# Decode attention on one core: 896 B of unused SBUF ahead of the tile that all loads write

## The chip, the cores and the metric

The kernel runs on one core of one Trainium2 chip. Its time is the device time of one execution in microseconds (us); three runs of the kernel before gave 1961.86, 1964.46 and 1965.69 us, with a median of 1964.46.

## The reference

Two independent attention blocks, A and B, each a decode step: one query token per sequence, two sequences, 32 heads with 192 elements each, and a cache of 8192 keys and values per head. The two outputs of 640 columns stand side by side. Everything is bf16.

```python
def _B_ref(x, k_cache, v_cache, wq, wo):          # x [2,1,640], caches [2,32,8192,192]
    B, Sq, D = x.shape
    H, Dh = 32, 192
    q = (x @ wq).reshape(B, Sq, H, Dh).transpose(0, 2, 1, 3)
    scores = jnp.einsum("bhqd,bhkd->bhqk", q, k_cache) * (Dh ** -0.5)
    p = _softmax(scores, axis=-1)
    o = jnp.einsum("bhqk,bhkd->bhqd", p, v_cache)
    return o.transpose(0, 2, 1, 3).reshape(B, Sq, H * Dh) @ wo
```

Block A computes the same with its own inputs. The four caches hold 201 MB each, so some 837 MB pass from DRAM through the core once, the weights included, and each value of a cache is used for one multiplication.

## The kernel before

**Units and loads.** A unit is one pair of heads of one sequence in one block: 64 units (`NU`). Its K (and likewise its V) is one load of 128 partitions x 128 tokens x 192 elements: the first head's 8192 tokens lie in partitions 0 to 63, the second head's in 64 to 127, so that each partition receives one contiguous row of 49152 B. A load is 6144 KB. SyncE issues all of them in one queue in the order K0, K1, V0, K2, V1, ... (`loads`), after the two query weights `wq` (61440 B per partition each). The output weights `wo` come at the end, in eight pieces (`pieces`), beside the last V, which is cut in three (`VCUT`).

**One tile holds everything that is loaded.** `big` (declared at line 136) is 172032 B in each partition: three buffers of 49152 B for K and V in turn (`kv`), and two buffers of 12288 B for products (`prod`). The weights `wq` and `wo` and the input x are loaded into the same bytes before and after they serve K and V. A buffer's next load waits until the load that lay in it has been used (`done`): a K until its last multiplication, a V until its last matmul.

**A unit's work.** VectorE multiplies a quarter of K by the unit's query (`dve_mul`, L280, four per unit, 128x6144 elements each) into a `prod` buffer. TensorE adds the 192 products of each token down to 16 partial sums with twelve matmuls against the identity (`pe_sum`, L352), and VectorE adds those 16 (`dve_red`, L283). GpSimd takes the maximum over the partitions (L261), ScalarE the exponential (L317), and TensorE multiplies the probabilities by V in 64 matmuls (`pe_pv`, L365). The queries are made at the start (L344), and the output projection (L387) runs at the end.

**Order.** Every engine's instructions are put in a table by unit (`put`) and emitted in that order; semaphores order the engines among each other. TensorE's steady part is a loop over six units.

**Places in SBUF.** Tiles are laid out in the order in which they are declared. Ahead of `big` lie 16384 B that the DMA machinery keeps and four small constants at 32 B each, so `big` begins at byte 16512 of each partition, which is 16 x 1024 + 128. Behind it come the queries (`qall`), the probabilities (`pb`), the scores (`sc`) and smaller tiles, up to byte 227944 of 229376.

The offsets inside `big` at which loads begin are multiples of 1024 B (the buffers at 0, 49152 and 98304; the second `wq` at 110592; pieces of `wo` at 30720, 20480, 10240 and 15360 from a buffer's start), save for the two small loads of x (at 100864) and the last piece of `wo` (at 17920 from a buffer's start), which begin 512 B past one.

Of the kernel before, what the change touches and what calls it, by code (L numbers as in the profile page):

```python
# [8 lines left out]
BF16 = mybir.dt.bfloat16  # L9
# [94 lines left out]
def build_kernel(nc, blocks, out):  # L104
# [26 lines left out]
    with ExitStack() as es:  # L131
        sb = lambda name, shape, dt: es.enter_context(nc.sbuf_tensor(name, shape, dt))
        ps = lambda name, shape, dt: es.enter_context(nc.psum_tensor(name, shape, dt))
        sem = lambda name: es.enter_context(nc.semaphore(name))

        big = sb("big", [128, NBUF * BUFE + 2 * PRODE], BF16)
        qall = sb("qall", [128, NU, Dh], BF16)
        pb = [sb(f"pb{i}", [128, TJ, MP], BF16) for i in range(2)]
# [389 lines left out]
def bass_concat_heads__gqa_block_cached__mha_block_cached__decode_kernel(  # L528
    nc: bass.Bass,
    A_x: bass.AP,  # L530
    A_k_cache: bass.AP,
    A_v_cache: bass.AP,
    A_wq: bass.AP,
    A_wo: bass.AP,
    B_x: bass.AP,
    B_k_cache: bass.AP,
    B_v_cache: bass.AP,
    B_wq: bass.AP,
    B_wo: bass.AP,
    out: bass.AP,  # L540
):
    blocks = [
        dict(x=A_x, k=A_k_cache, v=A_v_cache, wq=A_wq, wo=A_wo),
        dict(x=B_x, k=B_k_cache, v=B_v_cache, wq=B_wq, wo=B_wo),
    ]
    build_kernel(nc, blocks, out)
# [28 lines left out]
```

## Time and profile before

| what | value |
|---|---|
| median of three runs | 1964.46 us |
| the profiled execution | 1963.75 us |
| its span, first to last instruction | 1962.0 us |
| TensorE busy | 1527.6 us, 78% |
| VectorE busy | 1123.5 us, 57% |
| ScalarE, GpSimd busy | 160.3 and 31.3 us |
| read from DRAM | 836.77 MB, 426 GB/s over the span |
| mean granted TensorE clock | 0.949 |

Times of the profile count from the start of the span. A line of instruction groups gives the source line, the engine, the operation, what it writes and reads, and how often, then the busy time in us and the mean of one in ns. A line of a stretch gives its bounds and length, each engine's busy time with the number of instructions, the granted clock, the busy share of the 16 DMA engines and GB/s. A line of the chain or of the timeline begins with its start and its length in us. A chain is followed back from the last instruction: it names, for each moment, what the work that ended last was waiting for. A DMA in it lasts from its issue to its landing, queueing included.

### The profile page before, as it was taken

Reading aid. Unit: us, or ns where it says so; the run is one execution under the profiler, and the core shown is the slowest. Engines: PE = TensorE matmul, PEld = TensorE weight load, DVE = VectorE, ACT = ScalarE, POOL = GpSimd, SP = SyncE. Lnnn points to the kernel's source line nnn. Section 1 sums busy time; section 2 is a strip of 40 time slices with the busy share of each in tenths; the row PEclk is TensorE's granted clock in tenths of the full one; section 3 lists DMA queues with packets and bytes.
Section 4 is the critical chain, followed back from the end, with each engine's and each line's share of the span. In section 5 each row is a group of like instructions: output and inputs, shape, how many; then the busy total and the mean of one; then the engine's idle time right before and its main releaser. Section 6 shows DMA issues by size and latency. Waiting matters only on the chain.

```text
span 1962.0 us, 17861 instructions
## 1 busy us (share of the span) xinstructions
PE 1527.6 (78%) x7781; PEld 744.5 (38%) x7781; DVE 1123.5 (57%) x901; ACT 160.3 (8%) x519; POOL 31.3 (2%) x80
## 2 busy tenths in 40 slices
PE   4787877877877787777787787787787787777888
PEld 2343433333333333333333343343343343333345
DVE  3865565565565565566556556556556556556540
ACT  3100000000000000000000000000000000000000
POOL 1000000000000000000000000000000000000000
PEclk9999999999999988999998999999999898999899
DMA  9999999999999999999999999999999999999977
GB/s 396 433 433 432 433 432 432 433 433 433 431 433 433 433 433 433 433 433 433 433 432 433 432 433 433 432 433 433 433 434 433 433 433 433 433 433 432 433 332 327
DMA packets 20212, 837.12 MB, mean 427 GB/s; under 512 B 2252, under 2 KB 2264, under 8 KB 2648
## 3 DMA queue, kind: packets, MB, share of 16 engines
q1 hardware_dynamic: 20164, 836.77, 98.9%
q8 instruction: 13, 0.21, 0.0%
q14 instruction: 15, 0.12, 0.0%
q10 hardware_dynamic: 20, 0.01, 0.0%
HBM read 836.77 MB, written 0.01 MB: 426 GB/s over the span
## 4 chain that ended last, share of the span: by engine, by line
DMA 49%; PE 30%; DVE 20%; issue 0%; ACT 0%; SPq 0%
DMA big<-in_B_k_cache_dram 24%; DMA big<-in_A_k_cache_dram 22%; DVE big L280 17%; PE ops L365 17%; PE scps L352 11%; DVE sc L283 2%; DMA big<-in_B_wq_dram 2%; PE outps L387 1%; DMA big<-in_B_v_cache_dram 1%; PE scps L344 1%; PE ops L358 0%; PE oTps L374 0%; ACT out_sb L327 0%; SPq L235 0%; DVE mp L289 0%
## 5 line engine op out<-in xcount | busy, mean ns | idle before, releaser
L280 DVE TENSOR_TENSOR big<-big,qall 128x6144 bf16<-128x6144 bf16 x256 | 852.7, 3351 | 534.3 <-DMA big<-in_B_k_cache_dram 277.4
L352 PE MATMUL scps<-big,ident 128*128 128x512 bf16 x3072 | 782.2, 412 | 402.1 <-DVE big L280 402.1
L365 PE MATMUL ops<-big,pb 128*34 128x384 bf16 x4096 | 678.5, 327 | 3.7 <-DMA big<-in_B_v_cache_dram 3.7
L352 PEld LDWEIGHTS scps<-big,ident 128*128 128x128 bf16 x3072 | 304.0, 104 | 873.7 <-DVE big L280 497.8
L365 PEld LDWEIGHTS ops<-big,pb 128*34 128x34 bf16 x4096 | 396.0, 98 | 263.6 <-DMA big<-in_B_v_cache_dram 3.8
L283 DVE TENSOR_REDUCE sc<-scps 128x32 f32<-128x512 f32 x256 | 175.9, 687 | 206.6 <-PE scps L352 206.6
L309 ACT ACTIVATE nb<-mg 64x1 f32<-64x1 f32 x128 | 25.7, 201 | 1705.0 <-POOL mg L261 1704.3
L317 ACT ACTIVATE pb<-sc,nb 64x128 bf16<-64x128 f32 x128 | 81.7, 638 | 3.1
L261 POOL PARTITION_ALL_REDUCE mg<-mp x64 | 25.9, 405 | 1860.4 <-DVE mp L289 1860.4
L344 PE MATMUL scps<-big 128*128 128x384 bf16 x160 | 31.1, 364 | 14.5 <-DMA big<-in_A_wq_dram 11.0
L317 ACT ACTIVATION_READ_ACCUMULATOR pb<-sc,nb 64x1 f32 x128 | 38.5, 301 | 0.0
L289 DVE TENSOR_REDUCE mp<-sc 64x1 f32<-64x128 f32 x128 | 35.9, 280 | 3.1
L270 DVE CAST qall<-scps 64x192 bf16<-64x192 f32 x64 | 22.7, 355 | 19.5 <-PE scps L344 16.8
L303 ACT ACTIVATE qall<-o_sum,rc 2x192 bf16<-2x192 f32 x64 | 29.0, 454 | 18.1 <-DVE o_sum L300 16.4
L344 PEld LDWEIGHTS scps<-big 128*128 128x128 bf16 x160 | 17.1, 108 | 28.2 <-DMA big<-in_A_wq_dram 11.1
L387 PE MATMUL outps<-big,oTz 128*4 128x320 bf16 x192 | 26.6, 299 | 0.7 <-ACT out_sb L327 0.7
L294 DVE RECIPROCAL rc<-ops 2x1 f32<-2x1 f32 x64 | 10.0, 156 | 28.3 <-PE ops L365 26.3
L274 ACT ACTIVATE qall<-scps 64x192 bf16<-64x192 f32 x64 | 20.8, 325 | 34.4 <-DVE qall L270 32.2
L297 DVE COPY o_hi<-ops 2x192 f32<-2x192 f32 x64 | 22.3, 349 | 2.0
L300 DVE TENSOR_TENSOR o_sum<-ops,o_hi 2x192 f32<-2x192 f32 x64 | 22.1, 346 | 2.2
L387 PEld LDWEIGHTS outps<-big,oTz 128*4 128x4 bf16 x192 | 16.1, 85 | 10.7 <-issue 1.2
L358 PEld LDWEIGHTS ops<-ones,rs 128*2 128x2 f32 x128 | 5.5, 82 | 26.8 <-issue 26.7
(24 smaller groups left out, 42.0 us busy)
## 6 DMA issues: line engine op xcount, KB each, us to landing
big<-in_A_k_cache_dram SPq DMA_DIRECT2D x32, 6144.0 KB, 29.2
big<-in_A_v_cache_dram SPq DMA_DIRECT2D x32, 6144.0 KB, 28.1
big<-in_B_k_cache_dram SPq DMA_DIRECT2D x32, 6144.0 KB, 29.1
big<-in_B_v_cache_dram SPq DMA_DIRECT2D x31, 6144.0 KB, 27.9
big<-in_A_wq_dram SPq DMA_DIRECT2D x1, 7680.0 KB, 21.7
big<-in_B_wq_dram SPq DMA_DIRECT2D x1, 7680.0 KB, 39.8
big<-in_A_wo_dram SPq DMA_DIRECT2D x2, 3840.0 KB, 23.3
big<-in_B_wo_dram SPq DMA_DIRECT2D x2, 2560.0 KB, 32.1
```

Of the source, the lines that this page charges most:

```text
L261: return lambda eng: eng.partition_all_reduce(mg[u % 2][:], mp[u % 2][:], 128, bass.bass_isa.ReduceOp.max)
L270: return lambda eng: eng.tensor_copy(qall[ro, B * hp + 1 - s, :], qps[hp % NCH][ri, s * Dh:(s + 1) * Dh])
L280: return lambda eng: eng.tensor_tensor(prod[c % 2], t[:, c * TC:(c + 1) * TC, :], q, ALU.mult)
L283: return lambda eng: eng.tensor_reduce(sc[u % 2][:, c * TC:(c + 1) * TC], scps[c][:], AXL.X, ALU.add)
L289: ins = eng.tensor_reduce(mp[u % 2][r, s:s + 1], sc[u % 2][r, :], AXL.X, ALU.max)
L303: return lambda eng: eng.activation(qall[0:2, u, :], o_sum[:], ACTF.Identity, scale=rc[u % 2][:])
L309: ins = eng.activation(nb[u % 2][r, :], mg[u % 2][r, s:s + 1], ACTF.Identity, scale=-scale)
L317: ins = eng.activation(pb[u % 2][r, :, s::32], sc[u % 2][r, :].rearrange("p (j a) -> p j a", a=2), ACTF.Exp, bias=nb[u % 2][r, :], scale=s ...
L344: ins = eng.matmul(qps[hp % NCH][:, 0:QW], xbc[:, blk, c, :], wq_t[blk][:, c, off:off + QW], start=(c == 0), stop=(c == DC - 1))
L352: ins = eng.matmul(scps[c][:], ident[:], prod[c % 2][:, :, j * DG:(j + 1) * DG], start=(j == 0), stop=(j == NJ - 1))
L365: ins = eng.matmul(ops[u % 2][0:MP, 0:QW], pb[u % 2][:, j, :], vv[:, j, :], start=(j == 0), stop=(j == TJ - 1))
L387: ins = eng.matmul(outps[0:4, 0:NH2], oTz[blk][:, i, 2 - 2 * half:6 - 2 * half], wo[:, i - r0, half * NH2:(half + 1) * NH2], start=(i == 0 ...
```

## The change

One unused tile is declared ahead of `big`. It takes 448 bf16 elements, 896 B, in each partition. `big` then begins at byte 17408 = 17 x 1024, and all tiles behind it lie 896 B higher, the last one ending at byte 228840 of 229376. Nothing reads or writes the new tile.

```diff
@@ -133,6 +133,7 @@
         ps = lambda name, shape, dt: es.enter_context(nc.psum_tensor(name, shape, dt))
         sem = lambda name: es.enter_context(nc.semaphore(name))
 
+        shift = sb("shift", [128, 448], BF16)
         big = sb("big", [128, NBUF * BUFE + 2 * PRODE], BF16)
         qall = sb("qall", [128, NU, Dh], BF16)
         pb = [sb(f"pb{i}", [128, TJ, MP], BF16) for i in range(2)]
```

Every instruction stays in its place on its engine; only addresses in SBUF differ. The line numbers of the changed kernel are one higher.

## The prediction

> **What bounds the kernel now.** First the slices of the page, then the queue, then the stretches.
>
> ```profile
> DMA  9999999999999999999999999999999999999977
> GB/s 396 433 433 432 433 432 432 433 433 433 431 433 433 433 433 433 433 433 433 433 432 433 432 433 433 432 433 433 433 434 433 433 433 433 433 433 432 433 332 327
> ...
> q1 hardware_dynamic: 20164, 836.77, 98.9%
> ...
> 100.00:500.00 400.00, 310.06 (x1579) 150.31 (x1578) 238.31 (x178) 27.77 (x91) 4.63 (x13) 0.97 1.00 432
> 500.00:1000.00 500.00, 397.68 (x1970) 191.70 (x1969) 292.80 (x226) 38.44 (x126) 6.41 (x18) 0.94 1.00 433
> 1500.00:1800.00 300.00, 233.93 (x1149) 112.00 (x1150) 177.70 (x132) 21.36 (x70) 3.56 (x10) 0.94 1.00 433
> 1800.00:1900.00 100.00, 81.42 (x382) 37.74 (x380) 60.16 (x45) 6.41 (x21) 1.07 (x3) 0.91 0.90 385
> 1917.00:1962.00 45.00, 41.56 (x320) 25.59 (x320) 0.85 (x3) 1.44 (x4) 0.00 (x0) 0.96 0.75 319
> ```
>
> Each stretch ends with the granted clock, the DMA engines' busy share and GB/s. From 100 to 1800 us the 16 DMA engines are busy all the time and the rate lies at 432 to 433 GB/s, while TensorE is busy for 78 to 80% of it and VectorE for 59 to 60%. One queue, SyncE's, carries the whole load. Only behind the last K load, between about 1886 and 1898 us, do DMA engines fall idle, and again at the very end. The share of the chain (DMA 49%, PE 30%, DVE 20%) must not be read as half the time being compute. The chain shows why:
>
> ```profile
> 1618.46 28.90 DMA big<-in_B_k_cache_dram
> 1647.38 3.37 DVE big L280
> ...
> 1666.05 10.52 PE ops L365 x64
> 1676.59 28.90 DMA big<-in_B_k_cache_dram
> 1705.51 3.37 DVE big L280
> ...
> 1724.18 10.52 PE ops L365 x64
> 1734.71 28.90 DMA big<-in_B_k_cache_dram
> ```
>
> A K load is issued when TensorE has freed a buffer (1676.59) and lands 28.90 us later. Issues are 58.13 and 58.12 us apart, and in each such period four loads pass, so one takes 14.53 us; the other 14.4 us of the 28.90 are queueing behind the V load ahead of it. So the compute has a cover:
>
> ```profile
> 1605.01 0.33 SPq L235 DMA_DIRECT2D big<-in_B_v_cache_dram  x1
> 1618.46 0.33 SPq L235 DMA_DIRECT2D big<-in_B_k_cache_dram  x1
> 1634.92 0.33 SPq L235 DMA_DIRECT2D big<-in_B_v_cache_dram  x1
> ```
>
> The V load issued at 1634.92 can't start before the K load lands at 1647.36: it was issued 12.4 us early, the K load 14.4 us early. Engines that finish up to about 12 us later per 29 us change nothing here.
>
> **What one row costs.** The trace also records each DMA packet's bytes and time. A load is 128 rows, one packet each, 8 per DMA engine, and a 4 B packet that raises the semaphore. The 16256 rows of 49152 B took 1821.0 ns in the mean; 22% of them 1815 or less, 26% 1820 to 1821, and 4.6% 1826 or more (mostly 1827 and 1828). For the other sizes the commonest times are 102 ns (2560 B), 460 (12288 B), 912 (24576 B) and 2267 (61440 B). From the ends, (2267 - 102) / (61440 - 2560) = 0.03677 ns per byte, or 27.2 GB/s per engine and 435 GB/s for 16; what is left, 102 - 2560 x 0.03677, is 8 ns for a packet of any size. At 49152 B the bytes alone are 1807 ns, so everything that isn't bytes is 14 ns of 1821, or 0.8%: 8 ns fixed, 6 ns of small delays. That closes the account: 8 x 1821 ns is 14.57 us, and as a packet starts some 3 ns before the last one ends, it is within 0.03 us of the 14.53 of the chain.
>
> **The change, part by part.** The unused tile adds no instruction and no transfer; the same instructions stand in the same order on every engine, SyncE's queue included: 0 us. The tile `big` moves from byte 16512 to byte 17408 of each partition, and all tiles behind it move by the same 896 B. Before, 16512 = 16 x 1024 + 128, and each load starts 128 B past a multiple of 1024 (the last piece of `wo` and the two x loads 640 B past it); afterwards at a multiple of 1024 (these three: 512 B past it). So two costs could move.
>
> (1) The DMA write of a row. Rows that the DMA stage waits for: 127 whole K and V loads and two `wq` loads, 129 x 8 = 1032 per engine. No row of this trace writes from a multiple of 1024 B of SBUF, so the cost is bounded. Gain: if all 14 ns went, 1032 x 14 ns = 14.4 us. Loss: if each row became one of the dear 4.6%, 1827 instead of 1821, 1032 x 6 ns = 6.2 us. The nearest direct contrast lies in the output's stores: eight packets of 640 B. In the second half of the output, the two from ScalarE's queue go to addresses at 0 mod 256 and took 35 and 35 ns, and the two from SyncE's to addresses at 128 mod 256 and took 35 and 34. These are writes to DRAM, not to SBUF, but a destination 128 B off costs nothing there. Also, the 8 ns are found on the 4 B packets too (2251 of 2253 took 9 ns), which have no long row to misalign. I take 0 us.
>
> The rule that speaks for the change is in the Trainium skill, DMA: Bandwidth & Descriptors, section "How a descriptor splits into AXI transactions": a descriptor that doesn't start at a 256 B boundary begins with a transaction from the boundary below, and the unused bytes still cost beats. By it, 128 unused bytes per row would go if it holds for the write side, as in rival B. The output's stores do not bear this out for writes.
>
> (2) The engines' accesses to `big`, `qall`, `pb` and the rest. All of these move together by 896 B, so their positions to one another stay. Where the stage is DMA-bound, a slower access is covered by the 12.4 us above: L280 (3351 ns) runs four times between a K load's landing and the next issue, and would have to gain 3.1 us each before the DMA starves. Without cover are two stretches of the chain, 1880.8 to 1897.8 us (DVE and PE, until the last V load can be issued) and 1917.5 to 1960.3 (nearly all PE), 17.0 + 42.8 = 59.8 us. L280 and the matmuls at L352, L365 and L387 have no row at another address, so from both sides: if they ran a tenth faster or slower, a tenth of 59.8 is 6.0 us either way; I take 0, the case in which their relative places decide.
>
> Sum: 1963.75 us (the profiled execution: a span of 1962.0 and 1.7 around it) + 0 + 0 = 1963.75, which is 0.7 below the median of the runs, 1964.46. I forecast **1964 us**. A difference under 0.2% (3.9 us) is what the measurement of this kernel can't tell from none: its three runs span 3.8 us.
>
> **The rivals.**
>
> B, a little faster: each row wastes 128 B of line rate at its start. 128 x 0.03677 = 4.7 ns; 1032 rows make 4.9 us, and 40 further rows until the last V piece lands (three V pieces, two of `wo`) 0.2. 1964.46 - 5.0 = 1959.4 us, or 0.26%. For it: 8 ns fixed has room for 4.7. Against it: the stores above, and 1280 B rows of x, 128 off, at 53 and 55 ns, where the bytes are 47 and so the fixed part is 6 to 8, as it is on 4 B.
>
> C, clearly faster: the fixed part and the small delays both go. 1964.46 - 14.4 = 1950 us. For it: 14 ns is there. Against it: the 6 ns of delays are absent on most early rows (356 of the 434 that start before 90 us took 1815) and come later at the same addresses, so addresses alone don't make them.
>
> D, slower: rows that all begin at the same multiple of 1024 B meet in the memory of the partitions, in the main loop, and each waits as the dearest do now: 1827 ns, +6 ns, 1964.46 + 6.2 = 1970.7 us. It decides from +3.8 ns a row (3.9 us / 1032). For it: the delays grow once the loop runs, so something there is touched in common. Against it: the rows all start at one offset now too. The Trainium skill, SBUF — State Buffer, section "SBUF: two separate sides", says that DMA and engine accesses have ports of their own and cannot contend. By it this case falls away; the later growth from 1815 to 1820 ns leaves that open.
>
> E, slower by the engines: a tenth of the 59.8 us without cover, 1964.46 + 6.0 = 1970.5 us; it decides from 6.5% (3.9 of 59.8). Against it: nothing moves relative to anything else.
>
> That the change doesn't do what it says: it does for all but three small loads; if the address is without effect, that is my forecast.
>
> **How the numbers follow.** Chances: no change 0.48, B 0.20, C 0.08, D 0.17, E 0.07. The time is that of the likeliest, 1964 us, and its own range is 1961 to 1967. The range reaches to B and D and beyond them by about the scatter of the runs, 3.8 us, to each side: 1955 to 1974, with one more below because C lies there: 1954 to 1974. It leaves out most of C. Faster by over 0.2%: C's 0.08, some 0.14 of B (it lies just past the bound), 0.03 of the scatter: 0.25. Slower: most of D and E, 0.21, and 0.03: 0.24. Within 0.2%: 0.51.
>
> **What would show it.** The 49152 B packets at a mean of 1821 ns with the commonest times 1815 and 1820, loads 14.53 us apart, 432 to 433 GB/s from 100 to 1800 us, L280 at 3351 ns: all as before, if I am right. B: the commonest short rows at 1810 or 1811 ns instead of 1815. D: rows mostly at 1827. E: L280, L352 or L365 longer, the DMA's rows the same, and the loss only after 1880 us. A gap in the DMA between 100 and 1800 us would refute the reading of what bounds the kernel.

## The result and the profile after

The changed kernel takes 1958.08 us (median of six runs, 1956.22 to 1959.65) against 1964.24 for the kernel before on the same chip (six runs, 1961.86 to 1965.95). The ratio is 0.9971, with a 95% interval of 0.996 to 0.9982: 3.5 to 7.9 us less. The profiled execution took 1959.65 us with a span of 1957.9.

From the page before, the line of the multiplication:

```profile
L280 DVE TENSOR_TENSOR big<-big,qall 128x6144 bf16<-128x6144 bf16 x256 | 852.7, 3351 | 534.3 <-DMA big<-in_B_k_cache_dram 277.4
```

From the page after, the slices and the same line:

```profile
DMA  9999999999999999999999999999999999999987
GB/s 413 433 432 433 432 432 433 434 434 434 434 434 434 434 434 433 434 434 434 434 434 434 434 434 434 433 434 434 434 433 434 434 435 434 434 434 434 434 340 304
...
L281 DVE TENSOR_TENSOR big<-big,qall 128x6144 bf16<-128x6144 bf16 x256 | 852.8, 3352 | 524.0 <-DMA big<-in_B_k_cache_dram 275.1
```

And stretches of the same kernel, with each engine's busy time, the granted clock, the DMA share and GB/s:

```profile
100.00:500.00 400.00, 318.17 (x1597) 153.80 (x1596) 239.62 (x182) 29.89 (x98) 4.96 (x14) 0.95 1.00 434
500.00:1000.00 500.00, 397.80 (x1972) 191.41 (x1970) 291.23 (x221) 36.31 (x119) 6.02 (x17) 0.94 1.00 434
1500.00:1800.00 300.00, 238.25 (x1163) 113.74 (x1161) 177.56 (x133) 21.37 (x70) 3.54 (x10) 0.93 1.00 434
1800.00:1900.00 100.00, 80.31 (x409) 39.23 (x410) 58.48 (x49) 8.56 (x28) 1.42 (x4) 0.97 0.91 389
```

The DMA engines are as full as before (1.00), but in the same busy time they move 434 GB/s instead of 432 to 433. VectorE's multiplication is the same, 3352 ns against 3351. So the DMA stage itself became a little faster, and the multiplication did not. In the chain of waits after (start and length in us), the same loads come earlier:

```profile
216.85 27.92 DMA big<-in_A_k_cache_dram
...
1612.91 28.91 DMA big<-in_B_k_cache_dram
...
1670.75 29.08 DMA big<-in_B_k_cache_dram
...
1728.72 29.12 DMA big<-in_B_k_cache_dram
...
1890.87 19.78 DMA big<-in_B_v_cache_dram
1910.69 13.24 PE ops L366 x64
...
1933.19 8.29 PE outps L388 x48
1942.49 13.21 PE outps L388 x96
```

Issues lie 57.84 and 57.97 us apart, where they were 58.13 and 58.12. Three lines more of the chain of the kernel before make the account:

```profile
219.27 28.89 DMA big<-in_A_k_cache_dram
...
1917.49 12.21 PE ops L365 x64
...
1938.96 6.61 PE outps L387 x48
```

From one K load's issue to another's, 219.27 to 1734.71 before and 216.85 to 1728.72 after, the main loop took 1515.4 and 1511.9 us: 3.6 us less over 104 loads. Another 2.4 us lie ahead of that, in the head. By the last landing the changed kernel is 6.8 us ahead (1910.69 against 1917.49). Its last stretch, which is nearly all TensorE's, then took 2.7 us more in this execution, with 13.24 and 8.29 us where there were 12.21 and 6.61, while the granted clock was 0.90 from 1910 us on (0.96 before from 1917):

```profile
1917.00:1961.00 44.00, 41.56 (x320) 25.59 (x320) 0.85 (x3) 1.44 (x4) 0.00 (x0) 0.96 0.77 326
```

```profile
1910.00:1957.00 47.00, 44.27 (x320) 26.49 (x320) 0.85 (x3) 1.44 (x4) 0.00 (x0) 0.90 0.72 307
```

The trace's records of single DMA packets show what became faster. The 16256 rows of 49152 B:

```
            rows at 1815 ns or less   mean, ns   commonest times, ns
before                        21.7%     1821.0   1820, 1815, 1824, 1816
after                         99.5%     1815.8   1815
```

Some 0.2 to 0.3% of the rows take over 1.04 times the shortest, up to 4065 ns before (46 rows before, 27 of them in the first 100 us; 36 after, 17 of them there). Such rows are there in every kernel of this document, on a boundary and off it. Without them the mean was 1819.20 and is 1815.04. So the delays that came on top of 1815 ns were 4.20 ns a row and are 0.04: 4.16 x 1032 rows = 4.3 us. For the stretch of 104 loads this is 104 x 8 x 4.16 = 3.5 us, and the chain shows 3.6. The shortest row, 1815 ns, did not change at all. The smaller packets became alike too: of the 2560 B rows of `wo`, 152 of 256 took 102 ns before, and all 256 after, although half of these lie 512 B past a multiple of 1024.

The same packets give the time from load to load without the chain: from the start of the 17th K or V load to that of the 121st, again 104 loads, a load took 14.539 us before and 14.505 after. The 33 ns between them are eight rows of 4.2 ns, and over all 127 loads 4.3 us. The medians lie 6.2 us apart. The 1.9 us more don't show in this stretch; "Still open" below says what is known of them.

### The profile page after: what moved, and what is told of

Its sections match the earlier page's. It is cut to its first block, busy times and chain, and to the rows that moved or that the text cites. A ratio compares the mean times of both kernels' runs of the same rounds, so it can differ in the third digit from the quotient of the medians.

```text
span 1957.9 us, 17861 instructions
## 1 busy us (share of the span) xinstructions
PE 1534.4 (78%) x7781; PEld 747.0 (38%) x7781; DVE 1123.7 (57%) x901; ACT 160.3 (8%) x519; POOL 31.2 (2%) x80
## 4 chain that ended last, share of the span: by engine, by line
DMA 49%; PE 30%; DVE 20%; issue 0%; ACT 0%; SPq 0%
DMA big<-in_B_k_cache_dram 24%; DMA big<-in_A_k_cache_dram 22%; DVE big L281 18%; PE ops L366 17%; PE scps L353 10%; DVE sc L284 2%; DMA big<-in_B_wq_dram 2%; PE outps L388 1%; DMA big<-in_B_v_cache_dram 1%; PE scps L345 1%; PE ops L359 0%; PE oTps L375 0%; ACT out_sb L328 0%; SPq L236 0%; DVE mp L290 0%
## 5 line engine op out<-in xcount | busy, mean ns | idle before, releaser
L281 DVE TENSOR_TENSOR big<-big,qall 128x6144 bf16<-128x6144 bf16 x256 | 852.8, 3352 | 524.0 <-DMA big<-in_B_k_cache_dram 275.1
L345 PE MATMUL scps<-big 128*128 128x384 bf16 x160 | 29.4, 350 | 15.2 <-DMA big<-in_A_wq_dram 11.2
```

The costliest lines, as they stand in the source:

```text
L281: return lambda eng: eng.tensor_tensor(prod[c % 2], t[:, c * TC:(c + 1) * TC, :], q, ALU.mult)
L345: ins = eng.matmul(qps[hp % NCH][:, 0:QW], xbc[:, blk, c, :], wq_t[blk][:, c, off:off + QW], start=(c == 0), stop=(c == DC - 1))
```

## The experiments

All kernels here are the kernel before with the edit shown. "On" and "off" say whether the loads start at a multiple of 256 B. "Excess" is the mean time of all rows of K and V less the shortest common time, leaving out those over 1.04 times that, from the records of DMA packets. "Rows at it" is the share that took no longer than the shortest common time. The runs were made on several chips. Each ratio below is to the kernel before on the same chip, where its median was 1963.38 to 1964.93 us, and it compares the kernels better than the medians do.

```
kernel            row, B   shortest, ns   rows at it   excess, ns   median, us
before             49152           1815        21.7%         4.20   1964.24
behind             49152           1815        21.5%         4.22   1964.23
ahead_1024         49152           1815        21.1%         4.25   1963.38
off_64             49152           1815         8.3%         4.44   1963.45
after              49152           1815        99.5%         0.04   1958.08
ahead_128          49152           1815        99.5%         0.03   1958.45
ahead_384          49152           1815        99.0%         0.06   1958.51
loads_only_off     49152           1815        20.2%         4.30   1957.01
loads_only_on      49152           1815        99.7%         0.01   1949.54
quarters_off       12288            460        18.8%         4.02   1993.01
quarters_on        12288            460        99.8%         0.01   1975.54
both_off           48896           1806        19.8%         3.98   1954.55
read_off           48896           1806        99.2%         0.08   1949.93
end_off            49024           1811        73.6%         1.41   1956.79
```

**Is it the place of the loads, or of the other tiles?** In `behind` the unused tile stands after `big`, so that only the other tiles move:

```diff
         big = sb("big", [128, NBUF * BUFE + 2 * PRODE], BF16)
+        shift = sb("shift", [128, 448], BF16)
```

> The unused 896 B stand behind the large tile, so the loads write from 128 B past a multiple of 1024 as before, and all other tiles lie 896 B higher as in the changed kernel. Theory (the delays of the rows come from where a row's write starts): nothing is gained, 1964 us, 49152 B rows at a mean of 1821 ns with about a fifth at 1815. Rival (the other tiles' places matter: the queries, the probabilities, the scores): 1958 us and over 99% of the rows at 1815 ns.

Measured: 1.0003 of the kernel before (0.9994 to 1.0012), rows as before. The places of the queries, probabilities and scores are out.

**Any displacement?** `ahead_1024` has 512 elements ahead of `big`:

```diff
+        shift = sb("shift", [128, 512], BF16)
         big = sb("big", [128, NBUF * BUFE + 2 * PRODE], BF16)
```

> 1024 B ahead of the large tile: everything moves, and the loads still write from 128 B past a multiple of 1024. Theory: as before, 1964 us, rows at a mean of 1821 ns. Rival (any displacement of the tile, or its distance to what lies ahead, does it): 1958 us, rows at 1815 ns.

Measured: 1.0 (0.9991 to 1.0009), rows as before. Not the moving, but the place within the 1024 B counts.

**Which boundary?** `ahead_128`, `ahead_384` and `off_64` have 64, 192 and 32 elements in the same line.

> 128 B ahead: the loads write from multiples of 256 B, 256 B past a multiple of 512. Theory with 256 B as the boundary: all of the gain, 1958 us, rows at 1815 ns. Rival (the boundary is 512 or 1024 B): 1964 us and rows near 1821 ns, or something between, if the delay grows with the distance to the boundary.

Measured: 0.9975 (0.9965 to 0.9985) and 99.5% of the rows at 1815 ns. 128 B do what 896 B do.

> 384 B ahead: the loads write from multiples of 512 B, 512 B past a multiple of 1024. Theory with a boundary of 256 or 512 B: all of the gain, 1958 us, rows at 1815 ns; the last piece of the output weight, which lies at such a place in the changed kernel, took 102 ns in each of its 128 rows there. Rival (1024 B is needed): 1964 us.

Measured: 0.9968 (0.9955 to 0.9981), 99.0% at 1815 ns. From load to load, over the same 104 loads as above, `ahead_128` and `ahead_384` take 14.506 and 14.505 us like the changed kernel, `behind` and `ahead_1024` 14.539 like the kernel before.

> 64 B ahead of the large tile: the loads write from 192 B past a multiple of 256 B, 64 B off a multiple of 128. If only being off a boundary of 256 B counts: as before, 1964 us and rows at a mean of 1821 ns. If the delay follows the distance from the boundary below (192 B instead of 128, 7.1 ns of line rate instead of 4.7): rows near 1824 ns and some 1967 us.

Measured: 0.9999 (0.999 to 1.0009). The excess is 4.44 ns, not 7: it doesn't follow the distance. But the steps are others: 1818 ns is the commonest time (8175 of the 16256 rows), then 1825 (3103), where the 128 B offset gives 1820, 1815 and 1824. So 256 B is the boundary that is needed among those tried, and 192 B past it is about as bad as 128.

**Do the engines make the delays?** `loads_only_off` keeps all loads and waits and takes nearly all the work out:

```diff
-            return lambda eng: eng.tensor_tensor(prod[c % 2], t[:, c * TC:(c + 1) * TC, :], q, ALU.mult)
+            return lambda eng: eng.tensor_tensor(prod[c % 2][:, 0:1, :], t[:, c * TC:c * TC + 1, :], q[:, 0:1, :], ALU.mult)
...
-                for j in range(NJ):
+                for j in range(1):
...
-                for j in range(j0, j1):
+                for j in range(j0, j0 + 1):
```

(and each matmul starts and stops its own sum); `loads_only_on` has 128 B ahead of `big` as well.

> The loads are all there, in the same order and at the addresses of the kernel before (128 B off), with nearly no work behind them: each multiplication takes 1 of 32 tokens, each sum 1 of 12 matmuls, each product with V 1 of 64 matmuls (the cut ones 1 each). Theory that the delays arise among the DMA's own transfers: rows at a mean of about 1820 ns as with the work. Rival (the delays are collisions with the engines' reads and writes of SBUF, since they are rare before 120 us): nearly all rows at 1815 ns, and the same time as its twin on a boundary.

> The same with 128 B ahead of the large tile, so that all loads write from multiples of 256 B; the same work is left out. Rows at 1815 ns by both. By the theory that the DMA alone makes the delays this is 5 to 6 us shorter than its twin; by the rival the two are equal within 2 us.

One stretch of each, off and then on:

```profile
500.00:1000.00 500.00, 48.83 (x119) 10.34 (x119) 81.26 (x221) 36.22 (x119) 6.06 (x17) 0.50 1.00 433
```

```profile
500.00:1000.00 500.00, 48.84 (x119) 10.32 (x119) 81.28 (x221) 36.20 (x119) 6.03 (x17) 0.50 1.00 434
```

TensorE is busy for 49 of 500 us instead of 390 and more, VectorE for 81 instead of 291, and the rows off the boundary have the same excess, 4.30 ns; on it, 0.01. Against the kernel before the two take 0.9961 (0.9947 to 0.9975) and 0.9926 (0.9909 to 0.9942); the medians are 7.5 us apart, more than the 4.4 us of the rows (4.29 x 1032), but with these intervals the two don't contradict each other. From load to load the packets give 14.539 us off and 14.505 on, the same as with the work. The rival falls: the delays come with the place that the DMA writes to, whatever the engines do. In the kernel before too, a row's delay did not go with the multiplication: of the rows from 150 to 1800 us, those that lay wholly within multiplications of L280 had 4.34 ns, those with none beside them 4.42.

**By the row or by the byte?** `quarters_off` cuts each whole K or V load into four (and waits for four times the semaphore count); `quarters_on` adds 128 B ahead of `big`.

```diff
-                return [dma(t, src, (kind, u))]
+                return [dma(t[:, a:a + T // 4, :], src[:, a:a + T // 4, :], (kind, u)) for a in range(0, T, T // 4)]
```

> Each K or V load is cut into four of 32 tokens, so a row is 12288 B and there are four times as many starts, all 128 B off. If the delay is paid for each row's start: packets at about 465 ns where the shortest are 460, so 4 x 5 ns x 1016 = 20 us more than the twin on the boundary. If it is paid by the byte: about 461 ns and 5 to 6 us more than the twin. Both have the fixed 8 ns (5 ns once the overlap is taken off) three times more for each row: 15 to 25 us over the uncut kernels.

> The same cut into four with 128 B ahead of the large tile: every piece starts at a multiple of 256 B. Packets at 460 ns by both theories, 1958 us plus 15 to 25 us of fixed cost.

The same stretch of each, off and then on:

```profile
500.00:1000.00 500.00, 394.26 (x1926) 188.72 (x1924) 286.87 (x219) 36.29 (x119) 6.06 (x17) 0.92 1.01 426
```

```profile
500.00:1000.00 500.00, 396.17 (x1952) 189.90 (x1951) 292.72 (x225) 36.31 (x119) 6.06 (x17) 0.94 1.01 430
```

The difference is now 426 to 430 GB/s, nearly four times that of whole rows (by the packets 131 ns a load against 33). A quarter row has the excess of a whole one, 4.02 ns, and 4.01 x 4 x 1016 = 16.3 us; the medians are 17.5 us apart (ratios to the kernel before 1.0143, 1.0126 to 1.016, and 1.0057, 1.0041 to 1.0074). The price is by the row. On the boundary, cutting costs 17.1 us against the median of `ahead_128`. Three packets more for each of 1016 rows, at the fixed 8 ns less the 3 ns of overlap that the prediction found, would be 15.2 us of it; the three more semaphore packets of each load are not in this sum.

**Read, write, start or end?** In the last three, 128 B stand ahead of `big`, and each whole load leaves out 64 elements at one or both ends of its rows, so that read and write can be placed apart (the bytes that nothing else writes are zeroed once).

```diff
-                return [dma(t, src, (kind, u))]
+                tf, sf = t.rearrange("p t d -> p (t d)"), src.rearrange("p t d -> p (t d)")
+                return [dma(tf[:, 64:24512], sf[:, 64:24512], (kind, u))]      # both_off
+                return [dma(tf[:, 0:24448], sf[:, 64:24512], (kind, u))]       # read_off
+                return [dma(tf[:, 0:24512], sf[:, 0:24512], (kind, u))]        # end_off
```

> The large tile stands on a boundary of 256 B, and each whole K or V load leaves out the first 64 and the last 64 elements of its rows, so that it reads from 128 B off and writes to 128 B off. A row is 48896 B, for which the line of the packets gives 1806 ns (9.4 ns less than 1815, 9.6 us less in all). If the place of the write alone counts: delays as before, a mean near 1811 ns, 1954.5 us. If the write must only stand as the read does (both 128 B off): 1806 ns, 1948.5 us.

Measured: 1954.55 us, excess 3.98 ns. The ratio is 0.995 (0.9934 to 0.9967). That the read stands 128 B off like the write helps nothing.

> The same 48896 B per row, read from 128 B off (the same elements are left out) and written to a boundary of 256 B. If the place of the write alone counts: 1806 ns, 1948.5 us. If read and write must stand alike, or if the read's place counts too: delays, a mean near 1811 ns, 1954.5 us.

Measured: 1949.93 us, 0.993 (0.9911 to 0.9946), 99.2% of the rows at 1806 ns. Reading 128 B further on costs nothing. Of the two, the write's place alone counts.

> Each whole K or V load leaves out the last 64 elements of its rows: 49024 B, read and written from a boundary of 256 B, ending 128 B past one. The line of the packets gives 1811 ns, 4.8 us less in all. If the start alone counts: 1811 ns and 1953.3 us. If a row that ends inside 256 B is delayed too: a mean near 1815 ns, some 1958 us.

Measured: 1956.79 us, 0.9967 (0.9955 to 0.998), 3.5 above the one case and 1.2 below the other, so the time tells little. The rows tell more: 73.6% at 1811 ns, 1.41 ns of excess, a third of that of a row that is off at both ends. So a row that ends inside 256 B costs something too. It isn't the end of the read, which lies 128 B past a boundary in `read_off` as well. But the row's length is no multiple of 256 B either, and a length and an end of this kind weren't told apart. A write that starts off a boundary and ends on one wasn't tried; that the start costs the larger share, some 2.8 of 4.2 ns, is only the difference.

## Why the prediction was right, and where not

The range, 1954 to 1974 us, held the 1958.08, but the likeliest case, no change, was not the one that came. 0.29% faster lies just past the bound of 0.2% for no change, near rival B's 1959.4. That the range held it is no merit of the mechanism that was forecast: the range had been drawn out for the rivals, and "faster by over 0.2%" had a chance of only 0.25.

**What bounds the kernel** was read rightly. The DMA engines stayed busy from 100 to 1800 us, and a small gain in their rows came out as time; L281 took 3352 ns, where L280 had taken 3351.

**The failed step is (1), "The DMA write of a row", where I took 0 us.** It measured 4.16 ns a row, or 4.3 us. The value was chosen by the output's stores, four packets of 640 B that went to DRAM at 1961 us, when the last load had ended (1956.5 us). They say nothing of rows into SBUF behind one another, for which the stores were too far a row. The bounds of the same step, 14.4 us of gain and 6.2 of loss, did hold it. The loss was read a little too high: of the 753 rows at 1826 ns or more, 381 took 1826, and not mostly 1827 and 1828; 5 ns a row would be 5.2 us.

**Rival B** had the time nearly right and the mechanism wrong. It would have taken 4.7 ns off each row's fixed part, with the shortest rows at 1810 or 1811 ns. They stayed at 1815, and the fixed 8 ns is there on a boundary too (on it, a 12288 B packet takes 460 ns, 8 more than its bytes). What went is what C named the small delays: 4.2 of the 6 ns, of which the rest belongs to the few very long rows. That B came so near rests on 4.7 x 1032 and 4.16 x 1032 being alike.

The rule behind B, in the Trainium skill, DMA: Bandwidth & Descriptors, section "How a descriptor splits into AXI transactions", names the right boundary, 256 B: `ahead_128` got all that 896 B get. The size doesn't fit. By an estimate, its unused bytes at this trace's 0.03677 ns a byte, every row would pay the same 4.7 ns at 128 B and 7.1 at 192, and would pay them on the read; here a fifth of the rows at 128 B off had no delay, 192 B cost 4.44 ns, and reading 128 B further on cost nothing.

**The argument against rival C misled.** That the delays are absent on most early rows at the same addresses, "so addresses alone don't make them", is true as far as it goes: something else has to be there too. But it was read as evidence against the address, and the address is a condition: on a boundary, 99.5% of the rows took 1815 ns.

**Rival D** had the wrong sign, and **E** did not come: `behind`, where all tiles but `big` move, took the same time, and L281, which reads and writes the moved `big`, did too. (2) was right at 0. The 2.7 us that the last stretch took longer in the profiled execution came with a lower granted clock (0.90 against 0.96). It doesn't go with the address: from the start of the last whole load to the end of the span were 88.1 us before and 89.8 after, but 86.6 in `ahead_128` and 89.5 in `off_64`.

**Still open.** Why a write off the boundary is delayed, and why by these steps, no run shows. Nor is it known why the delays are rarer in the first 100 us or so (239 of the 354 rows from 90 to 130 us at 1815 ns before, 75 of 351 from 290 to 330): the same is seen with the main loop's work left out (246 of 355, then 41 of 353), so that work doesn't bring it about. It isn't that the 16 DMA engines begin in step and drift apart either, as far as the trace tells: 16 rows that start one after another from 60 us on already lie spread over 1.69 us, nearly the whole time of a row.

In every pair of kernels the medians differ by more than the rows do: 5.3 to 6.2 us against 4.3 for whole rows with the work, 7.5 against 4.4 without it, 17.5 against 16.3 for quarters, 4.6 against 4.0 in `both_off` and `read_off`. Between the 17th and the 121st load there is hardly any of it: at most 4 ns a load, or 0.5 us in all. The head's 2.4 us of the profiled execution don't go with the address: the 17th load began at 274.7 us before and 272.6 after, but at 272.9 in `behind`, where the loads write to the old place. So the profiled executions show scatter ahead of the main loop and behind it; that this makes the whole surplus is not shown.

## What to carry to other kernels

Where DMA engines are the bound, let each row of a load into SBUF begin at a multiple of 256 B of its partition, and end at one. An allocator that puts a few small constants first can spoil this for everything behind them, and a spare tile of 128 B mends it. The price of missing it was some 4 ns a row at both lengths tried: 0.3% of the time at rows of 49152 B, 0.9% at 12288 B. A row into DRAM is no stand-in for a row into SBUF, and a price that is missing from a profile should be bounded, not taken as 0 because a far row shows none.

## What the runs showed that was not expected

- The time of a row on a boundary is nearly without scatter: 16178 of the 16256 rows of the changed kernel took 1815 ns to the nanosecond, with all engines at work. What looked like noise of up to 13 ns was the offset.
- The delays come in steps that depend on the offset: most often 1816, 1820 and 1824 ns at 128 B past a boundary, 1818 and 1825 at 192 B past one.
- The engines' traffic to SBUF shows no price in the DMA's rows: the excess off the boundary is 4.20 ns with the work and 4.30 without it, and on the boundary 0.03 and 0.01.
